# A fused attention and two-layer kernel: tiles of 256 tokens instead of 384, keys stored zero-padded per head

## The chip, the cores and the metric

One core of one Trainium2 chip runs the program. The metric is device microseconds of one execution; three runs of the kernel before gave 310.33, 310.79 and 311.72 us, median 310.79.

## What is computed

Causal attention for 4 batches of 8 heads, 768 tokens, 64 columns a head. Retrieval heads see every earlier key; the other heads see the first 4 keys and a window of 64. The result, 3072 tokens of 512 columns, goes through two layers with h - tanh(h) between them.

```python
scores = scale * np.matmul(q, k.transpose(0, 1, 3, 2))
stream_keep = causal & (is_sink | in_win)
...
a = np.exp(scores)
a = a / (np.sum(a, axis=-1, keepdims=True) + 1e-09)
return np.matmul(a, v).astype(np.float32)
...
h = x @ w_in
g = h - np.tanh(h)
return (g @ w_out).astype(np.float32)
```

## The kernel before, in words

The tokens are cut into 8 tiles of TT = 384, two per batch. Attention runs in 32 units: unit n is one tile and one pair of heads. A unit has four stages. `st_T` (L213) transposes q and k of the pair on TensorE, three blocks each, into one PSUM tile `tp`, and a VectorE copy (L225) brings them to `qkT`, with head one of the pair on rows 0 to 63 and head two on rows 64 to 127. `st_S` (L246) multiplies keys by queries, each product on 64 of the rows (L259), in groups of up to 512 columns per head; ScalarE takes the exponential (L269), and VectorE multiplies the blocks near the diagonal by a 0/1 mask `m4` (L276, L277, L282). `st_A` (L289) multiplies by v, or by `vf`, v scaled by the flag of its head, for the blocks further off (L303), and VectorE divides by the row sum (L309, L311). `st_X` (L318) transposes the result into `xT` (L327).

The layers run on tiles too. `H_unit` (L334) makes one block of 128 of the 2048 hidden columns: four products `ph` (L341), a tanh on ScalarE (L346), and h - tanh(h) on VectorE into `gt` (L347). `O_mms` (L351) makes the output in strips of 128 tokens, 16 products `po` each (L356), evicted by ScalarE to `ot` (L363) and stored by SP's queue (L365). PSUM holds two `sc` tiles, which the transposes `tp` share, one `m` tile for `av` and `xp`, two `ph` and one `po`.

q and k come in by SP's queue, a whole tile per transfer (L81), in which each row takes three neighbouring tokens of a head, 768 bytes; `cast_qk` (L198) makes them 16 bit, on VectorE for the first two tiles and on POOL later. v (L95) and the weights (L109, L117) come through POOL's queue, which casts on the way; `far_v` (L186) makes `vf`.

The first tile's attention is made before the layers start (L390 to L406). From then on a plan (L413 to L441) spreads the stages of the next tiles over the steps of the layers: one step is an `H_unit` of tile t with three `O_mms` of tile t-1 (L443 to L454). The first tile of a batch gets 9 steps, the second 23. Each engine works through its instructions in order.

## Time and profile before

| | us |
|---|---|
| median of the runs | 310.79 |
| the profiled execution | 309.1 |
| its span, first to last instruction | 307.4 |
| TensorE busy | 250.5 |
| VectorE busy | 188.0 |
| ScalarE busy | 154.7 |
| POOL busy | 65.9 |

Busy time counts an instruction from its start to its end; matmuls overlap, so the distance between two starts tells what one costs in a stream. A wait is idle time of an engine, put down to what released it. The granted clock is the share of TensorE's full clock.

### The profile page before, as it was taken

How to read it: one execution, taken by the hardware profiler on the slowest of the kernel's cores; microseconds unless marked ns; L12 is line 12 of the kernel's file. 1: busy time of each engine (PE TensorE's matmuls, PEld its weight loads, DVE VectorE, ACT ScalarE, POOL GpSimd, SP SyncE). 2: the span in 40 equal slices, each digit the busy share in tenths (PEclk: the TensorE clock that was granted, in tenths of full speed). 3: DMA queues.
4: the chain of work that ended last, by engine and by line, in shares of the span. 5: the costliest groups of instructions: out<-in, count | busy, mean ns of one | idle time of the engine just before them, and what ended most of it. 6: DMA issues, size and time to landing. Idle time of an engine off the chain costs nothing.

```text
span 307.4 us, 5361 instructions
## 1 busy us (share of the span) xinstructions
PE 250.5 (81%) x2208; PEld 138.9 (45%) x2208; DVE 188.0 (61%) x329; ACT 154.7 (50%) x249; POOL 65.9 (21%) x75
## 2 busy tenths in 40 slices
PE   0012388998897999999689999999999999999984
PEld 0011253555454455555344555565455455554431
DVE  2449886777997465477886655667867455534300
ACT  1003126677565656755347666546485665344310
POOL 7108280445862002108520003000000000000000
PEclk9999996899999999999999999999999999999999
DMA  8999999694927100709300100000000010000111
GB/s 210 213 235 283 218 206 222 60 134 142 153 19 226 49 36 0 241 34 115 25 34 2 37 34 36 0 36 34 36 0 36 34 37 1 36 34 34 63 42 69
DMA packets 49449, 26.57 MB, mean 86 GB/s; under 512 B 25872, under 2 KB 46352, under 8 KB 49424
## 3 DMA queue, kind: packets, MB, share of 16 engines
q0 software_dynamic: 29184, 7.34, 24.6%
q1 hardware_dynamic: 20240, 18.89, 20.1%
q8 instruction: 17, 0.28, 0.4%
q14 instruction: 8, 0.07, 0.1%
HBM read 27.27 MB, written 6.29 MB: 109 GB/s over the span
## 4 chain that ended last, share of the span: by engine, by line
PE 51%; DVE 26%; ACT 10%; DMA 5%; issue 5%; SPq 1%; ACTq 0%
PE po L356 20%; PE ph L341 18%; DVE qkT L225 11%; PE sc L259 7%; ACT pt L269 6%; DMA raw_k<-in_k_dram 5%; PE av L303 4%; DVE gt L347 3%; DVE pt L276 3%; DVE x L311 3%; DVE pt L277 2%; ACT th L346 2%; ACT ot L363 2%; PE tp L221 2%; DVE m L180 1%
## 5 line engine op out<-in xcount | busy, mean ns | idle before, releaser
L269 ACT ACTIVATE pt<-sc 128x1024 f16<-128x1024 f32 x96 | 82.8, 918 | 64.1 <-PE sc L259 63.8
L341 PE MATMUL ph<-xT,win 128*128 128x384 f16 x512 | 109.3, 331 | 0.5 <-DVE gt L347 0.5
L356 PE MATMUL po<-wout,gt 128*128 128x512 f16 x384 | 105.3, 379 | 4.2 <-ACT ot L363 4.0
L347 DVE SCALAR_TENSOR_TENSOR gt<-th,ph 128x384 f16<-128x384 f32 x128 | 69.1, 546 | 51.3 <-ACT th L346 51.0
L346 ACT ACTIVATE th<-ph 128x384 f32<-128x384 f32 x128 | 63.1, 495 | 71.7 <-PE ph L341 68.2
L341 PEld LDWEIGHTS <-win 128*128 128x128 f16 x512 | 45.1, 99 | 30.8 <-issue 6.5
L356 PEld LDWEIGHTS <-gt 128*128 128x128 f16 x384 | 36.0, 98 | 36.0 <-issue 8.5
L259 PE MATMUL sc<-qkT 64*128 64x128 f16 (+2 forms) x352 | 32.0, 282 | 22.8 <-DVE qkT L225 15.0
L225 DVE COPY qkT<-tp 128x768 f16<-128x768 f16 x32 | 45.9, 1434 | 1.4 <-PE tp L221 1.3
L303 PEld LDWEIGHTS <-pt 128*128 128x128 f16 x672 | 29.0, 100 | 14.6 <-DVE pt L276 3.3
L259 PEld LDWEIGHTS <-qkT 64*128 64x128 f16 x352 | 14.4, 96 | 46.7 <-DVE qkT L225 19.2
L303 PE MATMUL av<-v,pt 128*128 128x65 f16 x352 | 28.8, 199 | 3.3 <-DVE pt L276 3.0
L282 DVE TENSOR_TENSOR pt<-pt,m 128x1536 f16<-128x1536 f16 x16 | 16.1, 1008 | 19.9 <-ACT pt L269 19.8
L95 POOL DMA_DIRECT2D v<-in_v_dram x24 | 21.7, 919 | 18.3 <-PE av L303 17.5
L221 PE MATMUL tp<-ident,t_q 128*128 128x128 f16 x96 | 11.6, 235 | 16.5 <-DVE ident L128 15.8
L303 PE MATMUL av<-vf,pt 128*128 128x65 f16 x320 | 24.0, 196 | 0.2
L201 POOL CAST t_q<-raw_q 128x1536 f16<-128x1536 f32 x6 | 9.5, 1580 | 57.4 <-PE tp L221 57.4
L363 ACT ACTIVATE ot<-po 128x512 f32<-128x512 f32 x24 | 14.4, 600 | 12.3 <-PE po L356 12.1
L190 POOL TENSOR_TENSOR vf<-v,rflag 128x520 f16<-128x520 f16 (+1 forms) x12 | 16.7, 1406 | 8.7 <-issue 8.2
L311 DVE TENSOR_TENSOR x<-av,rinv 128x384 f16<-128x384 f32 x32 | 17.7, 552 | 0.7
L221 PEld LDWEIGHTS <-t_q 128*128 128x128 f16 x96 | 8.4, 104 | 21.4 <-issue 10.0
L276 DVE TENSOR_TENSOR pt<-pt,m 128x1024 f16<-128x1024 f16 x16 | 11.9, 742 | 7.4 <-ACT pt L269 7.4
(37 smaller groups left out, 102.7 us busy)
## 6 DMA issues: line engine op xcount, KB each, us to landing
raw_q<-in_q_dram SPq DMA_DIRECT2D x8, 768.0 KB, 8.0
raw_k<-in_k_dram SPq DMA_DIRECT2D x8, 768.0 KB, 7.0
out_dram<-ot SPq DMA_DIRECT2D x24, 256.0 KB, 2.0
v<-in_v_dram POOLq DMA_DIRECT2D x24, 128.0 KB, 4.9
win<-in_moe_w_in_dram POOLq DMA_DIRECT2D x4, 512.0 KB, 14.6
wout<-in_moe_w_out_dram POOLq DMA_DIRECT2D x4, 512.0 KB, 9.4
retr_i<-in_is_retrieval_dram SPq DMA_DIRECT2D x1, 8.0 KB, 7.7
```

The lines of the kernel that those rows point to most:

```text
L95: nc.gpsimd.dma_start(out=v1s[b][:, :, i, 0:D], in_=v[b, :, i * 128 : (i + 1) * 128, :].rearrange("h p d -> p h d"),)
L221: nc.tensor.transpose(out=tp[:, g, i, :], in_=t16s[nm, t][:, i, 2 * hp : 2 * hp + 2, :], identity=ident16[:],)
L225: nc.vector.tensor_copy(out=qkT[b, hp][:, :, c * TT : (c + 1) * TT].rearrange("x g (p i) -> x g i p", i=NB), in_=tp[:],)
L259: nc.tensor.matmul(out=sc[:, hh, o : o + nb * 128], lhsT=qk[lo : lo + 64, 1, jb * 128 : jb * 128 + 128], rhs=qk[lo : lo + 64, 0, q0 * 128 ...
L269: nc.scalar.activation(out=pts[n][:, :, o0 : o0 + w], in_=sc[:, :, 0:w], func=AF.Exp, scale=inv_sqrt_d)
L276: nc.vector.tensor_mul(out=pt[:, :, 0:512], in0=pt[:, :, 0:512], in1=m4[:, hs, :])
L303: nc.tensor.matmul(out=av[:, i, hh, :], lhsT=pts[n][:, hh, co : co + 128], rhs=vv[:, h, jb, :], start=(x == 0), stop=(x == len(order) - 1),)
L311: nc.vector.tensor_mul(out=x16[:], in0=av[:, :, :, 0:D], in1=rinv[:].unsqueeze(3).to_broadcast([128, NB, 2, D]),)
L341: nc.tensor.matmul(out=ph[:], lhsT=w[:, cb, f0 : f0 + 128], rhs=xTs[t][:, cb, :], start=(cb == 0), stop=(cb == HP - 1),)
L346: nc.scalar.activation(out=th[:], in_=ph[:], func=AF.Tanh, scale=1.0 / XS)
L347: nc.vector.scalar_tensor_tensor(out=gts[t][:, fb, :], in0=th[:], scalar=-XS, in1=ph[:], op0=ALU.mult, op1=ALU.add)
L356: nc.tensor.matmul(out=pos[t][:], lhsT=gts[t][:, fb, ts * 128 : ts * 128 + 128], rhs=w_out_t[fb // 4][:, fb % 4, :], start=(fb == 0), stop ...
```

## The change

Tiles have 256 tokens, three per batch, 12 in all, and there are 48 units. q, k and v are loaded by SP's queue in natural token order, one transfer for 128 tokens of one of them, in pieces of 256 bytes (`load`); v is cast on POOL (`cast_v`). The first tile's q is cast on VectorE and its k on ScalarE, the second tile's both on VectorE, all later ones on POOL. Loads are issued two tiles ahead.

Keys are kept per batch in `kz`, a tile of 128 rows per head pair with one half per head: rows of the other head are zero. Two sets serve the batches in turn, zeroed once. `st_T` copies q whole and k in two halves of 64 rows; in `st_S` a product takes all 128 rows of `kz` and of `qT`. Groups of scores are evicted one at a time, and `st_X` of a unit is emitted one slot later, behind the first scores of the unit after next. A step of the layers is two hidden blocks of 256 tokens, with one tanh and one VectorE instruction for both, and four `po` products of tile t-1. The identity is made in 16 bit directly; the masks' last quarter is made after the first tile.

```diff
-TT = 384
+TT = 256
...
-    raw_pool = pool("raw", 4)
+    raw_pool = pool("raw", 6)
     t16_pool = pool("t16", 2)
-    qkt_pool = pool("qkt", 2)
+    qt_pool = pool("qt", 2)
...
+    NG = S // TT
     raws = {}
     v1s = {}
     vfs = {}
 
...
+    def load(t):
+        b, g = divmod(t, NG)
+        for nm, src in (("q", q), ("k", k), ("v", v)):
+            r = raw_pool.tile([128, NB, H, D], FP32, tag="raw", name=f"raw_{nm}{t}")
+            for i in range(NB):
+                s0 = g * TT + i * 128
+                nc.sync.dma_start(
+                    out=r[:, i, :, :], in_=src[b, :, s0 : s0 + 128, :].rearrange("h p d -> p h d")
+                )
             raws[nm, t] = r
...
-    load_qk(0)
-    load_v(0)
...
-    load_w_in(0)
+    load(0)
...
+    ident16 = select("ident16", 0, 1, -1, ALU.is_equal)
...
-    load_w_in(1)
-    ones_v(0)
+    load_w_in(0)
+
+
+    kz = [
+        [const.tile([128, 2, S], FP16, name=f"kz{s}_{hp}") for hp in range(HP)]
+        for s in range(2)
+    ]
+
+    def zero_kz(eng, s, hp, c0, c1):
+        eng.memset(kz[s][hp][:].bitcast(FP32)[:, :, c0 // 2 : c1 // 2], 0.0)
+
+    for hp in range(HP):
+        zero_kz(nc.vector, 0, hp, 0, TT)
...
+    def mask_head(h, c0, c1):
         nc.vector.scalar_tensor_tensor(
-            out=m4[:, h, :], in0=D4[:].rearrange("p a c -> p (a c)"),
-            scalar=rflag[:, h : h + 1], in1=S4[:].rearrange("p a c -> p (a c)"),
+            out=m4[:, h, c0:c1], in0=D4[:].rearrange("p a c -> p (a c)")[:, c0:c1],
+            scalar=rflag[:, h : h + 1], in1=S4[:].rearrange("p a c -> p (a c)")[:, c0:c1],
...
+    t16s = {}
+
+    def cast_qk(t, eq, ek):
+        for nm, eng in (("q", eq), ("k", ek)):
+            c16 = t16_pool.tile([128, NB, H, D], FP16, tag=f"t16{nm}", name=f"t16_{nm}{t}")
+            if eng is nc.scalar:
+                eng.copy(out=c16[:], in_=raws[nm, t][:])
+            else:
+                eng.tensor_copy(out=c16[:], in_=raws[nm, t][:])
+            t16s[nm, t] = c16
+
+    def cast_v(t):
+        b, g = divmod(t, NG)
+        if g == 0:
+            v1s[b] = v_pool.tile([128, 2 * NG, H, D + 1], FP16, tag="v1", name=f"v1_{b}")
+            vfs[b] = v_pool.tile([128, 4, H, D + 1], FP16, tag="vf", name=f"vf_{b}")
+        v1, vf, lo = v1s[b], vfs[b], g * NB
+        nc.gpsimd.tensor_copy(out=v1[:, lo : lo + NB, :, 0:D], in_=raws["v", t][:])
+        nc.gpsimd.memset(v1[:, lo : lo + NB, :, D : D + 1], 1.0 / XS)
+        for jb in range(lo, min(lo + NB, 4)):
+            fl = rflag0 if jb == 0 else rflag
             nc.gpsimd.tensor_mul(
...
+                out=vf[:, jb, :, :], in0=v1[:, jb, :, :],
+                in1=fl[:].unsqueeze(2).to_broadcast([128, H, D + 1]),
             )
...
+    def st_T(n, eq=None):
         t, hp = divmod(n, HP)
...
+        b, g = divmod(t, NG)
+        cs = slice(g * TT, (g + 1) * TT)
         tp = bank([128, 2, NB, 128], FP16, "sc", 2, f"tp{n}")
-        for g, nm in enumerate(("q", "k")):
+        for x, nm in enumerate(("q", "k")):
             for i in range(NB):
                 nc.tensor.transpose(
-                    out=tp[:, g, i, :], in_=t16s[nm, t][:, i, 2 * hp : 2 * hp + 2, :],
+                    out=tp[:, x, i, :], in_=t16s[nm, t][:, i, 2 * hp : 2 * hp + 2, :],
                     identity=ident16[:],
                 )
...
+        qT[n] = qt_pool.tile([128, TT], FP16, tag=f"qT{hp}", name=f"qT{n}")
+        tv = tp[:].rearrange("p x i c -> p x (i c)")
+        if eq is None:
+            nc.vector.tensor_copy(out=qT[n][:], in_=tv[:, 0, :])
+        else:
+            eq.copy(out=qT[n][:], in_=tv[:, 0, :])
+        kk = kz[b % 2][hp]
+        for hh in range(2):
+            ps_ = slice(64 * hh, 64 * hh + 64)
+            nc.vector.tensor_copy(out=kk[ps_, hh, cs], in_=tv[ps_, 1, :])
...
-        0: [[(0, 0, 2), (1, 1, 2)], [(2, 2, 1), (0, 2, 1)]],
-        1: [[(3, 3, 2), (4, 4, 2)], [(5, 5, 1), (2, 3, 3)], [(0, 3, 3), (3, 5, 1)], [(1, 3, 3)]],
+        0: [[(0, 0, 2), (1, 1, 1)]],
+        1: [[(2, 0, 2), (3, 1, 1), (1, 0, 1)], [(1, 1, 1), (0, 0, 2)]],
+        2: [[(4, 0, 2), (5, 1, 1), (3, 0, 1)], [(3, 1, 1), (0, 0, 2)], [(1, 0, 2), (2, 0, 2)]],
...
+    def st_S(n, gi):
         t, hp = divmod(n, HP)
...
+        b, g = divmod(t, NG)
+        if gi == 0:
+            pts[n] = pt_pool.tile([128, 2, 512 * NG], FP16, tag="pt", name=f"pt{n}")
+        pt = pts[n]
+        kk = kz[b % 2][hp]
+        sc = bank([128, 2, 512], FP32, "sc", 2, f"sc{n}_{gi}")
+        for hh in range(2):
             o = 0
...
+            for jb, q0, nb in GROUPS[g][gi]:
+                nc.tensor.matmul(
+                    out=sc[:, hh, o : o + nb * 128],
+                    lhsT=kk[:, hh, jb * 128 : jb * 128 + 128],
+                    rhs=qT[n][:, q0 * 128 : (q0 + nb) * 128],
+                    start=True, stop=True,
+                )
                 o += nb * 128
...
+        nc.scalar.activation(
+            out=pt[:, :, 512 * gi : 512 * gi + o], in_=sc[:, :, 0:o], func=AF.Exp, scale=inv_sqrt_d
+        )
+        if gi == 0:
             hs = slice(2 * hp, 2 * hp + 2)
...
+            if g == 0:
+                nc.vector.tensor_mul(out=pt[:, :, 0:384], in0=pt[:, :, 0:384], in1=m4[:, hs, 0:384])
             else:
-                pv = pt[:, :, 0:768].rearrange("p a (r c) -> p a r c", r=3)
+                pv = pt[:, :, 0:512].rearrange("p a (r c) -> p a r c", r=2)
                 nc.vector.tensor_mul(
                     out=pv, in0=pv,
-                    in1=m4[:, hs, 256:512].unsqueeze(2).to_broadcast([128, 2, 3, 256]),
+                    in1=m4[:, hs, 256:512].unsqueeze(2).to_broadcast([128, 2, 2, 256]),
                 )
 
...
+    def st_A(n, i):
         t, hp = divmod(n, HP)
-        b, c = divmod(t, 2)
-        if n not in avs:
+        b, g = divmod(t, NG)
+        if i == 0:
             avs[n] = bank([128, NB, 2, D + 1], FP32, "m", 1, f"av{n}")
         av = avs[n]
...
+        qb = g * NB + i
+        for hh in range(2):
+            h = 2 * hp + hh
+            for jb in range(qb + 1):
+                vv = v1s[b] if jb >= qb - 1 else vfs[b]
+                co = COL[g][jb, i]
+                nc.tensor.matmul(
+                    out=av[:, i, hh, :], lhsT=pts[n][:, hh, co : co + 128],
+                    rhs=vv[:, jb, h, :], start=(jb == 0), stop=(jb == qb),
+                )
...
-    def H_unit(t, fb):
-        if fb == 0:
+    FU = 2
+    NFU = NFB // FU
+
+    def H_unit(t, u):
+        if u == 0:
             gts[t] = g_pool.tile([128, NFB, TT], FP16, tag="gt", name=f"gt{t}")
...
+        ph = bank([128, FU, TT], FP32, "h", 2, f"ph{t}_{u}")
+        for j in range(FU):
+            fb = u * FU + j
+            f0 = (fb % 4) * 128
+            for cb in range(HP):
+                nc.tensor.matmul(
+                    out=ph[:, j, :], lhsT=w_in_t[fb // 4][:, cb, f0 : f0 + 128],
+                    rhs=xTs[t][:, cb, :], start=(cb == 0), stop=(cb == HP - 1),
+                )
+        th = th_pool.tile([128, FU, TT], FP32, tag="th", name=f"th{t}_{u}")
         nc.scalar.activation(out=th[:], in_=ph[:], func=AF.Tanh, scale=1.0 / XS)
         nc.vector.scalar_tensor_tensor(
-            out=gts[t][:, fb, :], in0=th[:], scalar=-XS, in1=ph[:], op0=ALU.mult, op1=ALU.add
+            out=gts[t][:, u * FU : (u + 1) * FU, :], in0=th[:], scalar=-XS, in1=ph[:],
+            op0=ALU.mult, op1=ALU.add,
...
+    def scores(n):
+        return [lambda gi=gi: st_S(n, gi) for gi in range(len(GROUPS[(n // HP) % NG]))]
+
+    def slot(n):
+
+        qs = scores(n + 1) if n + 1 < NU else []
         res = []
...
+        if qs:
+            res.append(qs.pop(0))
+        if n % HP:
+            res.append(lambda: st_X(n - 1))
+        res.append(lambda: st_A(n, 0))
+        if qs:
+            res.append(qs.pop(0))
+        res.append(lambda: st_A(n, 1))
+        res += qs
+        if n + 2 < NU:
+            res.append(lambda: st_T(n + 2))
+        if n % HP == HP - 1:
+            res.append(lambda: st_X(n))
         return res
 
-    NU = NTT * HP
-    cast_qk(0, nc.vector)
+    cast_qk(0, nc.vector, nc.scalar)
+    cast_v(0)
     for h in range(H):
...
+        mask_head(h, 0, 384)
+    load(1)
+    for j in (1, 2, 3):
         load_w_in(j)
...
+    for n in range(HP):
+        st_T(n, nc.scalar)
+        if n:
+            for f in scores(n - 1):
+                f()
+        if n > 1:
+            st_A(n - 2, 0)
+            st_A(n - 2, 1)
+        if n > 2:
+            st_X(n - 3)
+    for f in scores(HP - 1):
         f()
...
+    for n in (HP - 2, HP - 1):
+        st_A(n, 0)
+        st_A(n, 1)
+        st_X(n - 1)
+    st_X(HP - 1)
+
+    for h in range(H):
+        mask_head(h, 384, 512)
+    for hp in range(HP):
+        zero_kz(nc.gpsimd, 0, hp, TT, S)
+    cast_qk(1, nc.vector, nc.vector)
+    cast_v(1)
     for j in range(4):
         load_w_out(j)
+    load(2)
+    for hp in range(HP):
+        zero_kz(nc.gpsimd, 1, hp, 0, S)
 
 
     plan = {}
...
+    SPAN = {1: (0.0, 6.0), 2: (6.0, 16.0)}
+    for t in range(3, NTT):
+        lo = 16.0 + 24.0 * ((t - 3) // NG)
+        SPAN[t] = [(lo, lo + 3.4), (lo + 3.4, lo + 11.4), (lo + 11.4, lo + 24.0)][t % NG]
+    for t in range(1, NTT):
+        lo, hi = SPAN[t]
+        fs = []
         if t == 1:
...
+            fs += [lambda: st_T(HP), lambda: st_T(HP + 1)] + scores(HP)
         for hp in range(HP):
...
+            if hp == 1 and t + 2 < NTT:
+                fs.append(lambda t=t: load(t + 2))
             if hp == 0 and t + 1 < NTT:
...
+                fs.append(lambda t=t: cast_qk(t + 1, nc.gpsimd, nc.gpsimd))
+                fs.append(lambda t=t: cast_v(t + 1))
+            fs += slot(t * HP + hp)
         for i, f in enumerate(fs):
-            put(int(lo + (hi - lo) * i / len(fs)), f)
+            plan.setdefault(int(lo + (hi - lo) * i / len(fs)), []).append(f)
 
     for t in range(NTT):
...
+        for u in range(NFU):
+            fs = plan.get(t * NFU + u, [])
             half = (len(fs) + 1) // 2
             for f in fs[:half]:
                 f()
-            H_unit(t, fb)
+            H_unit(t, u)
             for f in fs[half:]:
                 f()
             if t:
-                O_mms(t - 1, 3 * fb, 3 * fb + 3)
+                O_mms(t - 1, 4 * u, 4 * u + 4)
     O_mms(NTT - 1, 0, NB * NFB)
 
 
```

VectorE at the end of the first tile's attention, before: `t16` are cast tiles, `x16` the divided results, `qkT` the copies of transposes of the second tile, `gt` the first layer output.

```order
L225 COPY qkT0_0_175<-tp4_373 128x2x3x128
L311 TENSOR_TENSOR x16_2_331<-av2_316,rinv2_329 128x384
L225 COPY qkT0_1_184<-tp5_390 128x2x3x128
L327 COPY xT0_249<-xp2_333 128x384
L309 RECIPROCAL rinv3_351<-av3_338 128x6
L311 TENSOR_TENSOR x16_3_353<-av3_338,rinv3_351 128x384
L282 TENSOR_TENSOR pt4_398<-pt4_398,m4_148 128x2x768
L327 COPY xT0_249<-xp3_355 128x384
L347 SCALAR_TENSOR_TENSOR gt0_381<-th0_0_387,ph0_0_382 128x384
```

The same place now:

```order
L317 COPY xT0_268<-xp0_269 128x256
L184 CAST t16_k1_329<-raw_k1_174 128x1024
L299 RECIPROCAL rinv2_288<-av2_281 128x4
L301 TENSOR_TENSOR x16_2_290<-av2_281,rinv2_288 128x256
L222 COPY qT4_361<-tp4_356 128x256
L228 COPY kz0_0_122<-tp4_356 64x256
L317 COPY xT0_268<-xp1_292 128x256
L228 COPY kz0_0_122<-tp4_356 64x256
L222 COPY qT5_370<-tp5_365 128x256
L299 RECIPROCAL rinv3_303<-av3_296 128x4
L228 COPY kz0_1_123<-tp5_365 64x256
L301 TENSOR_TENSOR x16_3_305<-av3_296,rinv3_303 128x256
```

The cast of the second tile's k now stands between the first tile's units, ahead of the results of its last two; before, the second tile's casts were long done here.

POOL at the start, before (`win` are the weights of the first layer):

```order
L95 DMA v1_0_101<-in_v_dram 128x8x64 x3
masks.py:197 MEMSET ident32_106 128x128
L109 DMA win0_115<-in_moe_w_in_dram 128x4x512
masks.py:199 ISA
masks.py:199 AFFINE_SELECT ident32_106<-ident32_106 128x128
L137 MEMSET ones_117 128x128
L109 DMA win1_127<-in_moe_w_in_dram 128x4x512
```

And now, behind `win0` and the selects:

```order
L194 MEMSET v1_0_157 128x16
L93 DMA win1_180<-in_moe_w_in_dram 128x4x512
L93 DMA win2_182<-in_moe_w_in_dram 128x4x512
L193 CAST v1_0_157<-raw_v0_105 128x16x64
L93 DMA win3_184<-in_moe_w_in_dram 128x4x512
L197 TENSOR_TENSOR vf_0_158<-v1_0_157,rflag0_138 128x520
```

The loads of v have left POOL's queue; three weight loads are issued before POOL waits for v.

VectorE between two units of the layers' stage, before:

```order
L309 RECIPROCAL rinv14_1555<-av14_1492 128x6
L311 TENSOR_TENSOR x16_14_1557<-av14_1492,rinv14_1555 128x384
L347 SCALAR_TENSOR_TENSOR gt2_1323<-th2_9_1564,ph2_9_1559 128x384
L225 COPY qkT2_0_1570<-tp16_1571 128x2x3x128
L327 COPY xT3_1294<-xp14_1587 128x384
```

And now:

```order
L299 RECIPROCAL rinv17_1455<-av17_1422 128x4
L301 TENSOR_TENSOR x16_17_1457<-av17_1422,rinv17_1455 128x256
L340 SCALAR_TENSOR_TENSOR gt2_1111<-th2_6_1444,ph2_6_1435 128x512
L222 COPY qT19_1468<-tp19_1463 128x256
L228 COPY kz1_3_129<-tp19_1463 64x256 x2
L340 SCALAR_TENSOR_TENSOR gt2_1111<-th2_7_1491,ph2_7_1482 128x512
L317 COPY xT4_1413<-xp17_1494 128x256
```

One scattering copy has become three plain ones, and `xT` has moved behind one more `gt`.

## Rows read from the trace of the kernel before

**Rows 1.** The page, part 1: busy time, share of the span, instructions.

```profile
PE 250.5 (81%) x2208; PEld 138.9 (45%) x2208; DVE 188.0 (61%) x329; ACT 154.7 (50%) x249; POOL 65.9 (21%) x75
```

**Rows 2.** Busy time by stage: stretch, length, engines (count), granted clock, DMA share, GB/s.

```profile
0.00:52.00 52.00, 17.03 (x151) 10.34 (x151) 33.50 (x52) 10.60 (x13) 21.84 (x34) 0.97 1.22 226
52.00:77.00 25.00, 23.12 (x259) 13.60 (x257) 17.87 (x30) 19.02 (x29) 11.93 (x11) 0.93 0.80 122
...
140.00:170.00 30.00, 25.62 (x242) 14.12 (x240) 22.70 (x38) 16.97 (x28) 11.31 (x11) 1.00 0.50 45
...
230.00:290.00 60.00, 58.73 (x446) 32.11 (x445) 29.61 (x56) 31.47 (x57) 0.00 (x0) 1.00 0.09 32
```

**Rows 3.** Timeline of TensorE at the end: start us, us, what.

```profile
299.30 3.61 PE L356 MATMUL po<-wout,gt 128*128 128x512 f16 x16 [0.69 <-ACT ot L363]
```

**Rows 4.** Timeline of TensorE in a paced stage, from 100 us on.

```profile
101.51 0.61 PE L259 MATMUL sc<-qkT 64*128 64x256 f16 x8
102.06 0.82 PE L341 MATMUL ph<-xT,win 128*128 128x384 f16 x4
...
105.77 0.55 PE L259 MATMUL sc<-qkT 64*128 64x384 f16 x6
106.25 0.82 PE L341 MATMUL ph<-xT,win 128*128 128x384 f16 x4
...
107.56 0.29 PE L303 MATMUL av<-vf,pt 128*128 128x65 f16 x4
107.69 0.23 PE L303 MATMUL av<-v,pt 128*128 128x65 f16 x2
...
109.24 0.33 PE L221 MATMUL tp<-ident,t_q 128*128 128x128 f16 x3
109.41 0.33 PE L221 MATMUL tp<-ident,t_k 128*128 128x128 f16 x3
...
111.04 0.81 PE L341 MATMUL ph<-xT,win 128*128 128x384 f16 x4
111.69 0.81 PE L356 MATMUL po<-wout,gt 128*128 128x512 f16 x3
112.34 0.81 PE L341 MATMUL ph<-xT,win 128*128 128x384 f16 x4
```

**Rows 5.** TensorE's waits from 52 to 303 us: total us, times, longest.

```profile
PE sc L259 <- DVE qkT L225: 5.9, 17, 0.6
PE xp L324 <- DVE x L311: 4.7, 4, 2.2
PE po L356 <- ACT ot L363: 4.0, 11, 0.7
```

**Rows 6.** Groups by line and shape: busy us, mean ns | idle before, releaser.

```profile
L347 DVE SCALAR_TENSOR_TENSOR gt<-th,ph 128x384 f16<-128x384 f32 x128 | 69.1, 546 | 51.3 <-ACT th L346 51.0
...
L225 DVE COPY qkT<-tp 128x768 f16<-128x768 f16 x32 | 45.9, 1434 | 1.4 <-PE tp L221 1.3
...
L311 DVE TENSOR_TENSOR x<-av,rinv 128x384 f16<-128x384 f32 x32 | 17.7, 552 | 0.7
...
L327 DVE COPY xT<-xp 128x384 f16<-128x384 f16 x32 | 10.9, 342 | 2.0 <-PE xp L324 2.0
...
L201 POOL CAST t_q<-raw_q 128x1536 f16<-128x1536 f32 x6 | 9.5, 1580 | 57.4 <-PE tp L221 57.4
...
L201 DVE CAST t_q<-raw_q 128x1536 f16<-128x1536 f32 x2 | 3.5, 1754 | 9.1 <-DMA raw_q<-in_q_dram 9.1
```

**Rows 7.** Three stretches: q, k loads; weight loads; v loads (columns as rows 2).

```profile
28.00:30.00 2.00, 1.22 (x12) 0.71 (x12) 2.00 (x4) 1.09 (x2) 1.74 (x3) 1.00 1.16 340
38.00:46.00 8.00, 6.49 (x60) 4.34 (x57) 6.43 (x11) 2.40 (x4) 7.02 (x8) 1.00 1.24 206
82.00:84.00 2.00, 1.54 (x15) 0.79 (x15) 2.00 (x5) 0.98 (x2) 1.45 (x3) 1.00 2.15 137
```

**Rows 8.** The chain of waits at the start: start us, us, what.

```profile
4.15 16.02 DMA raw_k<-in_k_dram
```

## What the change should do to the time

> **What bounds the kernel now.** Read the busy shares first: TensorE is busy for 250.5 of 307.4 us, VectorE for 188.0 [rows 1]. A share mixes stages, so next take the table by stage [rows 2]. Until 52 us TensorE is busy 17.0 us and VectorE 33.5: this is a stage of loads, masks and copies, in which the attention of the first tile is made. From 52 us the layers run; in 230 to 290 us TensorE is busy 58.7 of 60 us at a granted clock of 1.00, the upper level (2.4 GHz). So from 52 us until its last product, at 299.30 + 3.61 = 302.9 us [rows 3], TensorE paces the kernel, and two things count: when that stretch begins, and how much TensorE does and waits in it.
>
> What it does there comes from distances between starts, since the duration of a pipelined matmul holds latency [rows 4]. Four ph products (384 columns) start in 0.65 us, 162 ns each; three po products (512 columns) in 0.65 us, 216 ns each, or 0.422 ns a column; four av products in 0.13 us, 32 ns each; three transposes in 0.17 us, 56 ns each. Eight score products, 2048 columns, take 0.55 us up to the next ph; a plain stream at po's price would take 0.86 us. So the two heads of a pair, on different halves of the rows, do overlap. The six that follow (1792 columns) take 0.48 us.
>
> With the counts of the program: 512 ph 83.2 us, 384 po 83.1, 672 av 21.5, 288 transposes 16.2, and the scores: per batch and head pair 21 blocks per head of 128x128, 672 blocks in all; 30 of them take 0.55 + 0.48 = 1.03 us, so 23.1 us. Together 227.1 us, of which the first tile's attention, before 52 us, is 5.2 (48 score blocks 1.65, 48 av 1.5, 36 transposes 2.0). The stretch of 251 us thus holds 221.9 us of work and 29 us of waiting. The waits that the profile names there: 5.9 us for the copy qkT, 4.7 for x, 4.0 for the eviction ot [rows 5]; the rest is the latency that a stopped stream no longer overlaps, and the slower clock around 52 us (0.93 in 52 to 77 us) [rows 2].
>
> **The change, part by part.** *Scores.* The zero rows make each score product use all 128 rows, so two heads can no longer share the array. The columns stay 672 x 128 = 86,016; at 0.422 ns that is 36.3 us: **+13.2 us**, all but 0.3 of it on the path. The Trainium skill ("TensorE: Matmul & The Clock Gate", Part 3) says that products on distinct row groups run concurrently, starting some 4 ns apart. Taken alone that would put the old scores at half of 36.3 us and the loss at 18 us, the whole at some 309 us; the measured 1.03 us includes whatever a group costs at its ends, so the row decides and the rule gets no chance of its own.
>
> *Tile of 256.* ph becomes 768 products of 256 columns; on the line between 56 ns (128) and 162 ns (384) one is 109 ns, 83.9 us: **+0.7**. po, av and the transposes keep their counts. The first tile's attention, outside the stretch, shrinks from 5.2 to 3.4 us (24 blocks 1.3, 24 av 0.8, 24 transposes 1.3): **+1.8** inside. The output projection already ran one tile behind; nothing there. Work in the stretch: 221.9 + 13.2 + 0.7 + 1.8 = 237.6 us.
>
> *Waits.* The transpose of x is emitted a slot later, behind other scores (`slot`): the 4.7 us for x should go. The qkT copy, 1434 ns because it scatters the interleaved tokens [rows 6], becomes one copy of q and two of k of 256 plain columns; by xT (342 ns for 384) one is 228 to 342 ns, I take 280, so 0.83 us for the three. Its 5.9 us of waits fall to about 3.5. The ot waits stay (24 output tiles in both). What is late next is VectorE's other work between x and the scores; I add 1 us. 29 - 4.7 - 2.4 + 1 = **23 us**; bounds 15 (all three named waits gone) and 35 (the waits grow with 48 units instead of 32). Over the whole, VectorE's load stays: gt goes from 128 x 546 ns to 96 x about 680, so 70 to 65 us (728 ns in proportion, but part of the 546 is fixed), copies from 46 to about 39, while xT, x and the reciprocals gain some 15 calls each. ScalarE keeps the exponentials and saves 32 tanh calls. Both have room beside TensorE.
>
> *Loads.* q, k and v now come in pieces of 256 bytes on SP's queue, six transfers of 1024 pieces per tile. The trace has no such transfer. Nearest rows [rows 7]: loads of 1024 pieces of 768 bytes ran at 340 GB/s (28 to 30 us), 2.3 us each; v through POOL's queue, 1024 pieces of 256 bytes written as 128, at 137 GB/s, 0.96 us each; by bytes at 340 GB/s it would be 0.77 us. I take 1.3 us, nearer the v row, whose pieces have this size, with 0.77 and 2.3 as ends: 8 us a tile (5 to 14). In the stretch a tile lasts about 20 us and loads are issued two tiles ahead, so they hide, also where an output store waits ahead of one on SP. POOL casts q, k and v there, 3 casts of about 1.05 us by its 1580 ns for 1536 elements [rows 6], hidden in the same 20 us. Without that cover each late tile would cost its 8 us.
>
> *Start.* Here nothing hides them. Three w_in loads are issued on POOL before v is cast (before: two, behind v), each 512 KB at 206 GB/s [rows 7], 2.5 us. How such neighbours stretch a load: k of the second half was 16.0 us on the chain, from 4.15 to 20.2 us [rows 8]. I get: q at 7 us, k at 16 (5.2 us for q and k, 7.7 of weights between, latencies), v at 20; q and k of the second tile at 24 and 27, v of it at 30 to 38, since w_in and w_out loads share with it. VectorE, in order, has the cast of the second tile's k (1.2 us, 1024 of 1536 elements of 1754 ns [rows 6]) ahead of the last two units of the first tile; their copies take some 5 us more. So the layers start at 33 to 34 us, and av of the second tile, which stands early in TensorE's order, waits for v until up to 39. I set the start of the paced stretch at **36 us** (before: 52). Ends: 29 us, if loads are quick and only VectorE's masks and copies hold it; 47 us, if a transfer takes 2.3 us and k of the second tile lands at 41.
>
> *Sum*, against the profiled execution's own 309.1 us and span of 307.4: 36 + 237.6 + 23 + 4.5 (from the last product to the end, as now) = 301.1 us of span. Outside the span are 1.7 us, and the median of the runs, 310.79, lies 1.7 above the profiled execution: **304.5 us**.
>
> **Rivals.** *A, loads hold the start (slower).* The place is VectorE's cast of the second tile's k, behind which the first tile's last units are queued. Price: start at 47, span 312, 315.5 us. It decides from a start of 42.3 us on (span 307.4), between 1.3 and 2.3 us a transfer at about 1.75. For it: three weight loads now come sooner, and the count of pieces triples per byte. Against: the v row at 0.96 us. The Trainium skill ("DMA: Bandwidth & Descriptors", Specifications) wants 512 bytes at least for line rate; that speaks for A, and the v row, at 137 GB/s against 340, agrees that small pieces lose rate, though not that they cost as much as a large one.
>
> *B, VectorE takes over in each batch's first tile (no change).* There four units share 3.4 steps. A unit costs VectorE 0.83 us for the copies, 0.28 for xT, about 0.42 for x (552 ns for 384 [rows 6]) and no less for a mask; a step 0.68: at least 3.4 x 0.68 + 4 x 1.95 = 10.1 us. TensorE needs 3.4 x 1.74 (8 ph, 4 po) + 4 x 0.85 (6 blocks, 6 av, 6 transposes) = 9.3. The like stage before, 140 to 170 us, shows what that does: TensorE 25.6 of 30 us busy, VectorE 22.7 [rows 2]. Against it: the copies are shorter. If the waits stay at 29 us: span 307, 310.5 us.
>
> *C, quick loads (faster).* Start at 29 us, span 294, 297.5 us.
>
> *The full array buys nothing*: granted clock 1.00 in the paced stages says no clock is left to win. This is in the sum.
>
> **How the numbers follow.** Forecast 0.48, A 0.27, B 0.13, C 0.12. About 0.5% is what can be told from no change: 309.2 to 312.3 us. The forecast's own spread (waits 15 to 35, start 33 to 39) puts 0.43 of its 0.48 on faster and 0.04 on same, 0.01 on slower; C is all faster; B is 0.01 faster, 0.09 same, 0.03 slower; A slower. Faster 0.56, same 0.13, slower 0.31. The range 295 to 318 takes in A and most of C; the forecast's own is 299 to 309.
>
> **What would show it.** Right: score starts 56 and 108 ns apart, none at 4 ns; the xp waits gone and qkT's shorter; the layers starting near 36 us; TensorE's paced stretch longer, about 261 us. Wrong: q or k transfers over 1.75 us and VectorE idle before the second k cast (A); TensorE waiting over 29 us after the start with VectorE at nine tenths (B); score groups under 0.8 us for 2048 columns, which would sink the main term.

## The result, and the profile after

The changed kernel takes **290.91 us** (median of 4 runs, 288.61 to 291.32), the kernel before 310.84 beside it: a ratio of 0.934, 95% interval 0.929 to 0.939. Forecast were 304.5 us and a range from 295 to 318. Faster was right, the size was not: the gain is three times the one forecast. The profiled execution has a span of 289.6 us, 11.5 less than the sum's 301.1. Here and below a ratio compares the fast runs alone (those within 1.5% of the quickest of their kernel), with runs of the kernel before in the same session, whose medians lie between 309.4 and 311.0 us.

The page of the changed kernel, part 1 and the chain that ended last by engine, against [rows 1]:

```profile
PE 256.3 (89%) x2560; PEld 184.5 (64%) x2560; DVE 180.1 (62%) x463; ACT 154.3 (53%) x222; POOL 66.1 (23%) x86
...
PE 77%; DVE 8%; ACT 6%; DMA 5%; issue 2%; SPq 1%; ACTq 0%
```

The chain of the kernel before, which the prediction did not use, by engine and by line:

```profile
PE 51%; DVE 26%; ACT 10%; DMA 5%; issue 5%; SPq 1%; ACTq 0%
PE po L356 20%; PE ph L341 18%; DVE qkT L225 11%; PE sc L259 7%; ACT pt L269 6%; DMA raw_k<-in_k_dram 5%; PE av L303 4%; DVE gt L347 3%; DVE pt L276 3%; DVE x L311 3%; DVE pt L277 2%; ACT th L346 2%; ACT ot L363 2%; PE tp L221 2%; DVE m L180 1%
```

VectorE had 26% of the chain and has 8% now. The largest piece of the 26 was one copy, qkT: 11% of 307.4 us, some 34 us.

By stage (columns as in [rows 2]), the changed kernel:

```profile
0.00:36.00 36.00, 11.21 (x83) 7.34 (x84) 21.15 (x64) 7.40 (x11) 17.97 (x32) 1.00 1.06 188
36.00:60.00 24.00, 23.18 (x285) 18.68 (x284) 19.42 (x49) 18.56 (x26) 10.55 (x15) 1.00 1.13 215
60.00:100.00 40.00, 38.26 (x403) 27.62 (x400) 29.38 (x77) 23.29 (x34) 17.75 (x19) 1.00 0.83 173
100.00:260.00 160.00, 159.41 (x1653) 116.77 (x1651) 102.50 (x262) 96.17 (x140) 19.81 (x21) 1.00 0.23 60
```

The start is near where it was forecast: 36 us by these stages, and by the place in the program that the table below calls the begin 40.2 against 55.0, so 14.8 us sooner where 16 were forecast. Its casts, in the timeline (start us, us, what):

```profile
12.00 0.69 DVE L184 CAST t_q<-raw_q 128x1024 f16<-128x1024 f32 x1 [7.92 <-DMA raw_q<-in_q_dram]
...
19.45 1.04 ACT L182 CAST t_k<-raw_k 128x1024 f16<-128x1024 f32 x1
...
31.32 1.15 DVE L184 CAST t_k<-raw_k 128x1024 f16<-128x1024 f32 x1
```

In the table by stage, from 100 to 260 us TensorE is busy for 159.4 of 160 us. The same stretch before:

```profile
100.00:260.00 160.00, 150.15 (x1378) 83.83 (x1377) 102.05 (x185) 96.40 (x157) 19.02 (x17) 1.00 0.19 41
```

VectorE is busy for 102 us of it in both, so its load there did not fall. TensorE's waits from 36 us on (waited-for instruction, us in total, times, longest), against [rows 5]:

```profile
PE xp L314 <- DVE x L301: 1.4, 2, 0.9
PE po L350 <- ACT ot L357: 1.4, 2, 0.7
PE av L293 <- DVE xT L317: 0.6, 2, 0.5
PE sc L258 <- DVE kz L228: 0.3, 1, 0.3
```

And two groups that answer to [rows 6]; the prices taken for gt (about 680 ns) and for a copy of 256 columns (280) hold:

```profile
L340 DVE SCALAR_TENSOR_TENSOR gt<-th,ph 128x512 f16<-128x512 f32 x96 | 65.7, 685 | 27.0 <-ACT th L339 25.9
...
L228 DVE COPY kz<-tp 64x256 f16<-64x256 f16 x96 | 27.2, 283 | 4.7 <-ACT qT L224 3.2
```

### The profile page after: what moved, and what is told of

Read it like the earlier page. It is cut to its first block, busy times and chain, and to the rows that moved or that the text cites. A ratio compares the mean times of both kernels' runs of the same rounds, so it can differ in the third digit from the quotient of the medians.

```text
span 289.6 us, 6263 instructions
## 1 busy us (share of the span) xinstructions
PE 256.3 (89%) x2560; PEld 184.5 (64%) x2560; DVE 180.1 (62%) x463; ACT 154.3 (53%) x222; POOL 66.1 (23%) x86
## 4 chain that ended last, share of the span: by engine, by line
PE 77%; DVE 8%; ACT 6%; DMA 5%; issue 2%; SPq 1%; ACTq 0%
PE po L350 26%; PE ph L334 25%; PE sc L258 13%; PE av L293 7%; DMA raw_k<-in_k_dram 5%; ACT pt L265 4%; PE tp L215 3%; PE xp L314 2%; DVE pt L271 2%; DVE pt L274 1%; DVE gt L340 1%; ACT ot L357 1%; DVE x L301 1%; SPq L83 1%; DVE kz L228 1%
## 5 line engine op out<-in xcount | busy, mean ns | idle before, releaser
L265 ACT ACTIVATE pt<-sc 128x1024 f16<-128x1024 f32 (+1 forms) x96 | 86.9, 916 | 43.3 <-PE sc L258 42.4
L334 PE MATMUL ph<-xT,win 128*128 128x256 f16 x768 | 106.9, 274 | 0.0
L339 ACT ACTIVATE th<-ph 128x512 f32<-128x512 f32 x96 | 57.3, 597 | 55.7 <-PE ph L334 52.0
L340 DVE SCALAR_TENSOR_TENSOR gt<-th,ph 128x512 f16<-128x512 f32 x96 | 65.7, 685 | 27.0 <-ACT th L339 25.9
L334 PEld LDWEIGHTS <-win 128*128 128x128 f16 x768 | 71.8, 98 | 11.3 <-issue 0.2
L258 PE MATMUL sc<-qT,kz 128*128 128x128 f16 (+1 forms) x448 | 58.9, 255 | 2.0 <-DVE kz L228 1.2
L258 PEld LDWEIGHTS <-kz 128*128 128x128 f16 x448 | 37.7, 101 | 18.9 <-DVE kz L228 7.4
L274 DVE TENSOR_TENSOR pt<-pt,m 128x1024 f16<-128x1024 f16 x32 | 23.5, 733 | 16.6 <-ACT pt L265 16.2
L228 DVE COPY kz<-tp 64x256 f16<-64x256 f16 x96 | 27.2, 283 | 4.7 <-ACT qT L224 3.2
L193 POOL CAST v<-raw_v 128x1024 f16<-128x1024 f32 x12 | 13.2, 1098 | 50.6 <-DMA raw_v<-in_v_dram 40.2
L357 ACT ACTIVATE ot<-po 128x512 f32<-128x512 f32 x24 | 14.4, 598 | 12.4 <-PE po L350 12.4
L301 DVE TENSOR_TENSOR x<-av,rinv 128x256 f16<-128x256 f32 x48 | 20.2, 420 | 0.7
L215 PE MATMUL tp<-ident,t_k 128*128 128x128 f16 x96 | 13.6, 230 | 7.3 <-ACT t_k L182 7.2
```

The lines of the kernel that those rows point to most:

```text
L215: nc.tensor.transpose(out=tp[:, x, i, :], in_=t16s[nm, t][:, i, 2 * hp : 2 * hp + 2, :], identity=ident16[:],)
L228: nc.vector.tensor_copy(out=kk[ps_, hh, cs], in_=tv[ps_, 1, :])
L258: nc.tensor.matmul(out=sc[:, hh, o : o + nb * 128], lhsT=kk[:, hh, jb * 128 : jb * 128 + 128], rhs=qT[n][:, q0 * 128 : (q0 + nb) * 128], s ...
L265: nc.scalar.activation(out=pt[:, :, 512 * gi : 512 * gi + o], in_=sc[:, :, 0:o], func=AF.Exp, scale=inv_sqrt_d)
L274: nc.vector.tensor_mul(out=pv, in0=pv, in1=m4[:, hs, 256:512].unsqueeze(2).to_broadcast([128, 2, 2, 256]),)
L301: nc.vector.tensor_mul(out=x16[:], in0=av[:, :, :, 0:D], in1=rinv[:].unsqueeze(3).to_broadcast([128, NB, 2, D]),)
```

## The experiments

All times are medians of 4 runs or more, and the kernel before itself moved by 1.6 us between sessions; "gaps" below come from the trace of one execution, counted as follows. From the distance between two starts on TensorE the price of the first product is taken off (the prediction's prices, 0.109 us for 256 columns of ph); a score group is the distance from its first start to the next other product; what is left is a gap, put to the product that TensorE went to. The stretch runs from one 48th of the ph products (its begin) to the last po. The last column leaves out the waits between the last output strips, behind the last ph (2.5 us before, 1.7 in the changed kernel); the gaps column has them.

| kernel | begins, us | work | of it scores | gaps | ahead of scores | ahead of xp | ahead of po |
|---|---|---|---|---|---|---|---|
| before | 55.0 | 219.9 | 22.6 | 27.3 | 13.2 | 6.4 | 3.2 |
| before, straight copy | 49.5 | 220.3 | 23.1 | 17.7 | 5.9 | 4.2 | 3.5 |
| the same, 128-row scores | 49.4 | 229.9 | 32.6 | 12.6 | 1.6 | 3.5 | 3.4 |
| changed | 40.2 | 236.5 | 37.0 | 8.4 | 2.6 | 3.0 | -0.1 |
| changed, no zero rows | 40.1 | 227.5 | 28.0 | 16.2 | 9.8 | 2.5 | -0.1 |

Gaps shrank by 19 us, not by 6: that is the question. Theories: the scattering copy (T1), the later transpose of x (T2), the output strips that now end with a step (T5), or TensorE being slower at scores (the zero rows).

**The straight copy, in the kernel before.**

```diff
-            out=qkT[b, hp][:, :, c * TT : (c + 1) * TT].rearrange("x g (p i) -> x g i p", i=NB),
-            in_=tp[:],
+            out=qkT[b, hp][:, :, c * TT : (c + 1) * TT],
+            in_=tp[:].rearrange("x g i p -> x g (i p)"),
```

> The kernel before with its copy of the transposed q and k written straight instead of scattered (the tokens of a tile are then taken in another order, so that masks apply to other tokens; the amount of work is the same). Theory T1 (the long copy holds a score bank and VectorE, and the stretch pays it): the copy falls from 1434 ns to about 0.85 us, the gaps ahead of score groups shrink from 13.5 us to about 8, and the start, in which VectorE has eight of these copies, gets some 2 to 4 us shorter: 301 to 305 us. The prediction's own step gives -2.4 us: 308.4. Rival (hidden): 310 to 311.

293.43 us, ratio 0.945 (0.937 to 0.953): **in the kernel before, this one line is worth 17 us** by the medians and 15 by the profiled spans (307.4 to 292.5). That is no share of the change's 20 us: the change pays for its straight copies with smaller loads, and gains by other parts (see the sequence below). The group and the chain by engine:

```profile
L225 DVE COPY qkT<-tp 128x768 f16<-128x768 f16 x32 | 17.5, 549 | 0.1
```

```profile
PE 66%; ACT 11%; DVE 10%; DMA 6%; issue 4%; SPq 1%; ACTq 0%
```

The copy falls from 1434 ns to 549, not to 850; 32 times 0.885 is 28 us of VectorE. Of it 5.5 us show at the start (six copies stand ahead of the begin, 5.3 us) and 9.6 in the gaps: 7.3 ahead of scores and 2.2 ahead of xp, as x queues behind the copy on VectorE; ahead of po nothing went. A rival is TensorE's clock: in the profiled execution of before 0.87 were granted from 40 to 52 us and 0.93 from 52 to 77, here 1.00. But three executions of the kernel before with a mean granted clock of 1.00, in the same session, took 305.15, 309.06 and 312.15 us, so the clock is not what made the difference. The Trainium skill ("VectorE: DVE Perf Modes", "Mode 2×_1P — pack two bf16 into one 32-bit read") lets 16-bit operands go two at a time only where neighbours are adjacent. The trace agrees in direction: the stride of three elements costs a factor of 2.6. That is more than the factor of two between two at a time and one, and what makes the rest is not shown.

**The scattering copy, in the changed kernel.** `qT` and `kz` are written with a stride of two.

```diff
+        iv = lambda a: a.rearrange("p (c i) -> p i c", i=NB)
...
-            nc.vector.tensor_copy(out=kk[ps_, hh, cs], in_=tv[ps_, 1, :])
+            nc.vector.tensor_copy(out=iv(kk[ps_, hh, cs]), in_=tv[ps_, 1, :, :])
```

> The changed kernel with its three copies of the transposed q and k writing every second element, as the copy before wrote every third (the tokens of a tile are then taken in another order, so that masks apply to other tokens; the amount of work is the same). Theory T1 (the long scattering copy that holds a score bank was behind most of the waits of before, beyond the 5.9 us named): the copies get slower by about half (before 1.87 ns an element against some 1.1 now), and 4 to 8 us come back: 295 to 299 us. Rival (the copies are hidden here, the waits went by other parts of the change): within 1.5 us of the changed kernel, 290 to 292.5.

298.0 us, ratio 0.960 (0.953 to 0.967): 7 us back, within the 4 to 8 of T1, but for the most part by another way.

```profile
L229 DVE COPY kz<-tp 64x256 f16<-64x256 f16 x96 | 42.2, 439 | 5.2 <-ACT qT L225 3.6
...
L223 DVE COPY qT<-tp 128x256 f16<-128x256 f16 x44 | 19.4, 440 | 7.5 <-PE tp L215 7.4
```

156 ns more on each of 140 copies, 22 us of VectorE, and yet the gaps of the stretch are 10.7 us instead of 8.4. The other 5.9 us are lost at the start: the stretch begins at 46.1 instead of 40.2 us. There VectorE works in another order than in the changed kernel, where the last masks (m) were done by 27.4 us and the cast of the second tile's q came at 29.47, in 0.66 us. Here two masks and that cast run beside POOL's instructions, and TensorE waits 4.5 us for the cast:

```profile
31.84 2.67 DVE L170 SCALAR_TENSOR_TENSOR m<-D,rflag,S 128x128 f16<-128x128 f16 x2
32.02 2.07 POOL L197 TENSOR_TENSOR vf<-v,rflag 128x520 f16<-128x520 f16 x2
34.03 2.77 POOL L139 MEMSET kz<- 128x768 f32 x4
34.52 2.83 DVE L184 CAST t_q<-raw_q 128x1024 f16<-128x1024 f32 x1
37.41 0.61 PE L215 MATMUL tp<-ident,t_q 128*128 128x128 f16 x4 [4.52 <-DVE t_q L184]
```

So in the changed kernel this run shows 2 us in the gaps for T1; the start's share comes with the order and the overlap, and is not the copies' own price.

**Strips that end with a step; x a slot later; all three.** In the kernel before:

```diff
+    J = [0]
+    for m in (3, 3, 3, 3, 2, 2, 3, 3, 3, 3, 4, 3, 3, 3, 3, 4):
+        J.append(J[-1] + m)
...
-                O_mms(t - 1, 3 * fb, 3 * fb + 3)
+                O_mms(t - 1, J[fb], J[fb + 1])
```

> The kernel before with one edit: the output products of a step are 3,3,3,3,2,2,3,3,3,3,4,3,3,3,3,4 instead of 3 each, so that the 16 products of an output tile always end with a step, as four a step do in the changed kernel, and never in the middle of three. Theory T5 (the ot waits are there because the next output tile's first product stands right behind the last product of the one before, in the only bank): 3.2 us of gaps inside output products go, 307.5 to 309 us, and ot is no longer among TensorE's waits except at the tail. Rival (the wait moves to the next thing): no change, 310 to 311.5.

307.3 us, ratio 0.991 (0.981 to 1.000): not told from no change, though the named ot waits fall from 4.0 us to 2.4. For x:

```diff
+        if late and n % HP:
+            if qs:
+                res.append(qs.pop(0))
+            res.append(lambda: st_X(n - 1))
```

> The kernel before with the transpose of x moved one slot later, behind the next unit's first scores, from the second tile on. The prediction's step gives -4.7 us: 306 us. Rival, after the same move undone in the changed kernel made no difference (289.84 against 290.91 us): what waited for x waits at the next instruction instead: within 1.5 us, 309.5 to 312.

312.41 us, ratio 1.007 (0.998 to 1.015): no gain. From 52 us on, in a profiled execution of 313.95 us:

```profile
PE sc L259 <- DVE qkT L225: 9.3, 15, 2.9
PE po L356 <- ACT ot L363: 3.8, 10, 0.7
...
PE xp L324 <- DVE x L311: 0.7, 1, 0.7
```

The x wait is all but gone (4.7 to 0.7), and the next one, for qkT, stands at 9.3 where it was 5.9: as this one trace has it, the lateness of VectorE is met one instruction later.

> The three edits of the kernel before together: straight copy, output products that end with a step, transpose of x a slot later. If the waits of the paced stretch are these three, its gaps fall from 28.5 us to about 15 (4.3 us of them are the entries into the 64-row score groups, 0.095 us each, which only the zero rows take away; 1.7 are the tail) and the time to 294 to 300 us. If they are one pool of lateness of VectorE in which any one edit gives most: about as the best single one of the three.

292.54 us, ratio 0.940 (0.932 to 0.948), 0.9 under the straight copy alone, within both intervals. The second reading holds.

**The same move undone in the changed kernel** (`st_X(n)` at the end of its own slot).

```diff
-        if n % HP:
-            res.append(lambda: st_X(n - 1))
...
-        if n % HP == HP - 1:
-            res.append(lambda: st_X(n))
+        res.append(lambda: st_X(n))
```

> The changed kernel with the transpose of x put back at the end of its own slot. Theory T2 (moving it one slot later removed the x waits): 3 to 6 us come back, 294 to 297 us, with xp waits of some 4 us. Rival (with two sub-blocks per unit, x is early enough anyhow): within 1.5 us of the changed kernel.

289.84 us, ratio 0.932 (0.926 to 0.938): nothing, as the rival said. T2 falls in both kernels.

**Without the zero rows.**

```diff
-            for jb, q0, nb in GROUPS[g][gi]:
+        for jb, q0, nb in GROUPS[g][gi]:
+            for hh in range(2):
+                lo = 64 * hh
...
-                    lhsT=kk[:, hh, jb * 128 : jb * 128 + 128],
+                    lhsT=kk[lo : lo + 64, jb * 128 : jb * 128 + 128],
```

> The changed kernel with the zero rows taken out: k kept once per head pair, score products of 64 rows in adjacent pairs, one k copy instead of two, no zeroing; everything else stays. The prediction priced the zero rows at +13.2 us, so by that step about 290.9 - 13 = 278 us, with the waits as small as in the changed kernel. By the rule of full overlap it would be 18 us, 273. Rival: the waits are small in the changed kernel because TensorE is slowed by the full-array products and VectorE has more time; then waits come back as TensorE gets shorter, and the time is 283 to 291 us.

290.0 us, ratio 0.934 (0.930 to 0.938): **the zero rows cost 0.9 us or nothing, not 13**, and that with their second copy of k and their zeroing, which this run leaves out too. TensorE's timeline, first without zero rows (64-row products), then the changed kernel:

```profile
106.61 1.03 PE L344 MATMUL po<-wout,gt 128*128 128x512 f16 x4
107.48 0.28 PE L308 MATMUL xp<-ident,x 128*128 128x128 f16 x2
...
108.46 1.03 PE L344 MATMUL po<-wout,gt 128*128 128x512 f16 x4
109.42 0.40 PE L252 MATMUL sc<-qT,kz 64*128 64x256 f16 x6
109.75 1.05 PE L328 MATMUL ph<-xT,win 128*128 128x256 f16 x8
```

```profile
108.99 1.03 PE L350 MATMUL po<-wout,gt 128*128 128x512 f16 x4
109.86 0.60 PE L258 MATMUL sc<-qT,kz 128*128 128x256 f16 x6
110.30 1.04 PE L334 MATMUL ph<-xT,win 128*128 128x256 f16 x8
```

Four po take 0.87 us up to an xp, but 0.96 up to a 64-row score; into 128-row scores they take 0.87 again. Over all groups the median delay at the entry is 0.095 us, against 0.000. The group of 1024 columns then takes 0.33 us instead of 0.44, and one of 2048 took 0.55 before [rows 4]: 0.22 us per 1024 columns and 0.11 fixed, put here to the exit. So a stay (a run of 64-row products between other ones) costs 0.205 us besides its columns, and by an estimate from these numbers pairs win only beyond some 970 columns in a stay. Units of the changed kernel have groups of 768 and 1024. The Trainium skill ("TensorEngine Tiling (Array Packing)", "Key Properties") says that a change of tiling mode drains TensorE. The trace agrees, as far as a delay at the entry shows it, and gives the price.

**128-row scores alone**, on the kernel before with the straight copy; both heads' rows enter each product.

```diff
-                        lhsT=qk[lo : lo + 64, 1, jb * 128 : jb * 128 + 128],
-                        rhs=qk[lo : lo + 64, 0, q0 * 128 : (q0 + nb) * 128],
+                        lhsT=qk[:, 1, jb * 128 : jb * 128 + 128],
+                        rhs=qk[:, 0, q0 * 128 : (q0 + nb) * 128],
```

> The kernel before with the straight copy, and score products that take all 128 rows, so both heads' rows at once (a head's scores are then the sum of the two heads' scores; the number of products and columns is the same, and no copy is added). It prices the full array alone, against 293.4 us of the straight copy. The prediction's step: +13.2, 306.6 us. With the entries into 64-row products (0.095 us each at some 48 groups, booked as waits in the prediction) taken off: +8.7, 302 us. Rival (TensorE waits so often at score groups that the slower products lie in its waits): within 2 us of 293.4.

298.29 us, ratio 0.959 (0.952 to 0.966), 4.9 above the straight copy. The table has both sides: scores +9.5 us in the stretch, gaps -5.1, of which 4.3 are some 45 entries.

**Fewer stays** (first two groups of a unit back to back, on the kernel without zero rows).

```diff
-        if qs:
+        if len(qs) > 1:
+            a, b = qs.pop(0), qs.pop(0)
+            res.append(lambda: (a(), b()))
+        elif qs:
             res.append(qs.pop(0))
```

> The kernel without zero rows (pairs of 64-row products) with the first two score groups of a unit emitted back to back, so that TensorE goes into the 64-row products 64 times instead of 96. Theory: each stay in 64-row products costs a fixed 0.2 us (0.095 at its entry, 0.11 at its end) besides 0.211 ns a column, which is why the pairs won nothing in the changed kernel's small groups (290.0 against 290.9 us). Then 32 stays fewer give -6.5 us: 283.5 us. Rival: two groups in a row need both score banks free, and what is saved comes back as waits for the exponentials or the copies: 288 to 292 us.

289.35 us, ratio 0.927 (0.918 to 0.936), 0.7 under the kernel without zero rows and not told from it. Score groups fell from 28.0 to 23.9 us as meant; gaps rose from 16.2 to 18.0. Since its stretch also began later, 43.9 instead of 40.1 us, this run doesn't settle what grouping is worth.

**Natural order alone**, tiles of 384: three loads per q and k in pieces of 256 bytes, and the straight copy.

```diff
-                out=r[:].rearrange("p h i d -> p h (i d)"),
-                in_=src[b, :, c * TT : (c + 1) * TT, :].rearrange(
-                    "h (p i) d -> p h (i d)", i=NB
-                ),
+                    out=r[:, i, :, :],
+                    in_=src[b, :, s0 : s0 + 128, :].rearrange("h p d -> p h d"),
```

> The kernel before with natural token order alone, as the change has it: q and k loaded in pieces of 256 bytes (three transfers each instead of one), plain cast, straight copy; tiles of 384, pairs of 64-row products, and all else as before. The straight copy alone gave 293.4 us with pieces of 768 bytes. If the small pieces are hidden except at the start, where three transfers of 1024 pieces take the place of one, the start gets 2 to 5 us later: 295 to 299 us. Rival: the start is held by masks, copies and weights, not by q and k: 293 to 294.5.

302.08 us, ratio 0.974 (0.967 to 0.980). The straight copy is worth 17 us, and loads in three transfers of small pieces take back 8.7, all of it before the first quarter of the ph products is done (111.8 us against 101.7).

**Loads of the changed kernel.** Pieces of 512 bytes, then one w_out load for four:

```diff
+                out=r[:].rearrange("p h i d -> p h (i d)"),
+                in_=src[b, :, g * TT : (g + 1) * TT, :].rearrange("h (p i) d -> p h (i d)", i=NB),
```

> The changed kernel with q, k and v loaded in pieces of 512 bytes, one transfer of 1024 pieces instead of two (a partition then holds two neighbouring tokens; the copies stay straight, so the tokens of a tile are taken in another order and masks apply to other tokens). If the small pieces cost the changed kernel what they cost the kernel before (8.7 us for three tiles' worth at the start), the first 55 us shrink by 4 to 8 us: 283 to 287 us. Rival: the first 55 us are held by the weights' casting loads, which run at some 200 GB/s whatever the pieces beside them, or by VectorE: within 2 us of 290.9.

294.66 us, ratio 0.954 (0.948 to 0.960): slower, and so inconclusive. q landed at 5.8 us instead of 12.0 and k at 10.3 instead of 18.2, but VectorE, in order, held the cast of the second tile's q ahead of the masks, which started at 17.34 instead of 13.87 us and took 5.93 us instead of 4.32:

```profile
13.70 0.69 DVE L183 CAST t_q<-raw_q 128x1024 f16<-128x1024 f32 x1 [7.21 <-DMA raw_q<-in_q_dram]
...
17.34 5.93 DVE L169 SCALAR_TENSOR_TENSOR m<-D,rflag,S 128x384 f16<-128x384 f16 x8
23.20 1.22 DVE L227 COPY kz<-tp 64x256 f16<-64x256 f16 x4
```

```diff
-    for j in range(4):
-        load_w_out(j)
+    load_w_out(0)
+    w_out_t.extend(w_out_t * 3)
```

> The changed kernel with the first w_out load standing in for all four (three of eight weight loads are left out, 3 MB of reading; the output uses the first quarter of w_out four times). If the bytes loaded hold the first 55 us, the third tile's q, k and v land earlier and some 3 to 6 us go: 285 to 288 us. Rival: nothing waits for loads after the second tile in the changed kernel itself: within 1.5 us of 290.9.

291.06 us, ratio 0.943 (0.937 to 0.948): the time does not wait for w_out's bytes.

**The start.** A load of weights waits for k by a copy of one column into its tile:

```diff
+        if j:
+            nc.gpsimd.tensor_copy(out=w[:, 0, 0:1], in_=raws["k", 0][:, 1, H - 1, 0:1])
...
+    nc.scalar.activation(out=warm[:], in_=ones[:, 0:1], func=AF.Exp)
...
-    cast_qk(0, nc.vector, nc.scalar)
+    cast_qk(0, nc.scalar, nc.scalar)
```

> The changed kernel with a start that lets q and k of the first tile go first: the second to fourth w_in loads and the w_out loads are issued only after k of the first and of the second tile has landed, the activation table is loaded at the beginning, and q is cast on ScalarE, so that VectorE makes its masks while the loads run. If loads shared with the weights held the start (36 us), k lands near 11 to 13 us instead of 18 and the layers start near 30 to 32: 285 to 287 us. Rival: what is saved on k is paid by the weights and the second tile's loads, which then land as late or later: no change, or up to 2 us slower.

290.28 us, ratio 0.936 (0.931 to 0.942). k landed at 11.2 us, yet the layers' stretch began 2 us sooner only: VectorE made masks of the second tile (4.5 us at 14.44) before it applied the first tile's, and the second tile's k came at 26.5. Then one of VectorE's products with a mask ran beside POOL's `vf` and took 3.52 us, where the next took 0.68, and TensorE waited for the copy behind it:

```profile
31.22 3.52 DVE L279 TENSOR_TENSOR pt<-pt,m 128x1024 f16<-128x1024 f16 x1 [0.34 <-ACT pt L270]
31.58 2.07 POOL L202 TENSOR_TENSOR vf<-v,rflag 128x520 f16<-128x520 f16 x2
34.99 1.22 PE L339 MATMUL ph<-xT,win 128*128 128x256 f16 x5 [2.71 <-DVE xT L322]
```

**Together.** Pairs with the first two groups in a row, one copy of q and k per unit, and that start with all masks first:

```diff
-        nc.vector.tensor_copy(out=qT[n][:], in_=tv[:, 0, :])
-        nc.vector.tensor_copy(out=kk[:, cs], in_=tv[:, 1, :])
+        nc.vector.tensor_copy(out=kk[:, :, cs], in_=tv)
...
+        mask_head(h, 0, 512)
```

> What the runs point to, together: tiles of 256 in natural order, pairs of 64-row products with the first two groups back to back, one straight copy of q and k per unit instead of three, and a start in which the second to fourth w_in loads wait for k of the first and second tile and the w_out loads for k of the second, q and the first tile's copies go through ScalarE, and all masks are made while the loads run. Fewer stays -6.5, the copy 0.85 to about 0.4 us a unit (VectorE, worth some 2 us), the start some 5 to 8 us sooner: 273 to 279 us. Rival: if the grouping gives nothing and the start only the 2 us that the earlier start experiment showed: 285 to 289.

282.93 us, ratio 0.909 (0.900 to 0.918). The layers began 7 us sooner and stood again for the third tile's loads; stretches of 2 us, clock in the third column from the end:

```profile
40.00:42.00 2.00, 0.47 (x6) 0.44 (x7) 0.14 (x1) 0.00 (x0) 1.04 (x1) 1.00 1.21 196
42.00:44.00 2.00, 2.00 (x30) 1.46 (x28) 1.48 (x4) 0.48 (x1) 0.00 (x0) 0.62 1.22 196
44.00:46.00 2.00, 2.00 (x15) 1.15 (x13) 1.12 (x3) 1.74 (x3) 0.00 (x0) 0.53 1.22 196
46.00:48.00 2.00, 2.00 (x29) 1.55 (x26) 1.17 (x4) 1.51 (x2) 0.00 (x0) 1.00 1.21 215
```

The wait ahead of them, in TensorE's timeline:

```profile
41.53 0.28 PE L216 MATMUL tp<-ident,t_k 128*128 128x128 f16 x2 [3.78 <-POOL t_k L185]
```

After 3.8 us without work the granted clock is 0.62 and 0.53, so mostly the lower level (1.2 GHz), until 46 us. So the weights were loaded as float32 on SP's queue, in the order of need, and cast on GpSimd:

```diff
-        nc.gpsimd.dma_start(
-            out=w[:],
+        s = st_pool.tile([128, HP, 512], FP32, tag="stg", name=f"swin{j}")
+        nc.sync.dma_start(
+            out=s[:],
...
+        nc.gpsimd.tensor_copy(out=w[:], in_=s[:])
```

> The combined kernel (282.93 us) with its weights loaded as float32 on the same queue as q, k and v, in the order in which they are needed, the third tile's q, k and v ahead of w_out, and cast on GpSimd (about 2.1 us a load by 1038 ns for 1024 elements, eight loads). If the rate of the casting loads (some 200 GB/s) and their order hold its first 55 us, where TensorE waits 3.8 us for the third tile's k and 2.5 us for its v with the granted clock down to 0.5 to 0.7 for some 2 to 4 us after each, those go: 273 to 279 us. Rival: q, k and v then stand behind weights in one queue and GpSimd's casts are late: 283 to 288.

**279.69 us, ratio 0.907 (0.900 to 0.913)**, the lowest median here, though by the ratios not told from the run before it (0.900 to 0.918). Its first two stages:

```profile
0.00:30.00 30.00, 14.27 (x126) 7.92 (x126) 20.18 (x46) 13.19 (x18) 14.99 (x25) 1.00 1.08 260
30.00:60.00 30.00, 26.86 (x332) 18.37 (x333) 21.08 (x44) 20.36 (x29) 16.11 (x11) 1.00 0.97 261
```

The clock stays at 1.00. The 260 GB/s against 192 in the first 60 us of the run before it are no faster transfer: the views count bytes as written, and a casting load writes half of what it reads. The weights there and here (KB each, us to landing):

```profile
win<-in_moe_w_in_dram POOLq DMA_DIRECT2D x4, 512.0 KB, 8.4
swin<-in_moe_w_in_dram SPq DMA_DIRECT2D x4, 1024.0 KB, 7.8
```

With the 4.2 MB that eight casting loads read and do not write, both kernels read some 15.7 MB in their first 60 us. What differs is the order: the third tile's k lands at 35.4 us instead of 40.2 and its v at 37.3 instead of 50.3, and TensorE's waits for them (3.8 and 2.5 us) are gone.

## Why the prediction was wrong, point by point

- **Start, 36 us: right, within about a microsecond.** k landed at 18.2 us (16 foreseen) and the cast of the second tile's k came at 31.3. Rivals A and C did not occur; B neither. One reading was off: the 137 GB/s of the v row count bytes written, half of what those casting loads read, so most of its distance to 340 is the cast and not the small pieces. The price of 1.3 us went by the row's time and is not touched.
- **Waits, 23 us: the step that failed.** With the start and the work of the sum, the measured span leaves 11.5 us of waits. The prediction cut 6 us of 29; in the stretch above the gaps fell by 18.9, from 27.3 to 8.4. It took the copy's worth from the one line of waits that names it, 5.9 us, and left 3.5 of them, so 2.4 us. In the kernel before, the straight copy alone took 9.6 us of gaps: all of the named 5.9, some 2 that the wait list books under x, and the rest under no name. A copy of 1.4 us holds up what stands behind it on VectorE too. The chain gave 11% of the span, 34 us, as its ceiling. Another 4.3 us were entries into 64-row products, which the sum had among its waits and kept (see the scores). The remaining 5 us lie mostly ahead of po and xp. These amounts come from different kernels, so they add up only roughly.
- **x a slot later, -4.7 us: wrong in its cause.** The gaps ahead of xp went from 6.4 to 3.0 us, but the move is worth nothing in either kernel (two runs).
- **ot, kept at 4.0 us: wrong in the row, little in the time.** Ahead of po the gaps went from 3.2 to none, since 16 is a multiple of 4 and not of 3; the like cure in the kernel before, which left 2.4 of the 4.0 us of named waits, gave 0.9%, with 0 to 1.9% in its interval.
- **Scores, +13.2 us: the size held, the reckoning did not.** Scores grew by 14.4 us in the stretch. But on the kernel before, with the straight copy, the full rows cost 4.9 us in the time, not 13.2: 4.3 us of what the prediction called waits were entries into 64-row products, which full rows remove. In the changed kernel's small groups the two prices cancel: 9.0 us of scores against 7.8 of gaps, 0.9 us in the time.
- **Tile of 256** (ph 109 ns apart, +0.7) **and end** (4.0 us after the last po, 4.5 taken): right.

In sequence, by the runs: 310.7 us before; 302.1 with natural order (straight copy, small loads); 290.0 with tiles of 256, the steps of four and the x move, which is mostly the start (the stretch begins at 40.1 instead of 51.1 us); 290.9 with zero rows. The step from 302.1 to 290.0, which the prediction had in its start, gave more than the copy and its loads together.

## What to carry to other kernels

Take the wait that bears an operation's name as a floor of what it costs, and its share of the chain as a ceiling: here 5.9 and 34 us, and 15 to 17 measured, in one case. Write 16-bit copies straight where the loads allow it: one strided index cost that much of 310 us, and the small loads that came with its removal took half of it back. Use pairs of half-height products only in stays long enough to pay for entry and exit, here some 970 columns. A wait removed by moving an instruction is met again at the next one if the engine behind it is what is late.

## What had not been expected of the hardware

- A copy of 768 16-bit elements from PSUM took 549 ns straight and 1434 ns with a stride of three; 256 elements took 283 ns straight and 439 with a stride of two.
- Entry into 64-row products cost 0.095 us and the exit 0.11, in groups of 768 to 2048 columns alike; between 128-row products of different kinds it was 0.000.
- Some of VectorE's instructions from SBUF to SBUF took several times as long while POOL was at work: a cast 2.83 us instead of 0.66, a product with a mask 3.52 instead of 0.68. That is read from their overlap in the traces; no run tried it alone.
